# A new order of all pieces of work in a fused attention and MLP kernel

## The chip, the cores and the metric

The kernel runs on one core of a Trainium2 chip. The time is the device time of one execution in microseconds (us); the lowest, the median and the highest of three runs are given. A core has five engines with a queue of instructions each: PE (matrix products; its weight loads are listed as PEld), DVE (vector), ACT (scalar functions), POOL and SP, which here only issues transfers. Each engine works through its queue strictly in order, and an instruction that waits for another engine or for a transfer holds up all that stands behind it on its own queue.

## The reference

One normalised input feeds two branches, and their sum is added to the input. The rest of the function is plain: `x` is 2048 x 512, there are 32 heads of 16, and four segments of 512 rows.

```python
xn = _layernorm(x, axis=-1)
return x + _A_ref(xn, A_wq, A_wk, A_wv, A_wo, A_beta) + _B_ref(xn, B_w1, B_w2)

# _A_ref, for each of 4 segments s
logits = jnp.einsum('bhqd,bhkd->bhqk', qs, ks) * scale + mask
a_dot = jnp.einsum('bhqk,bhkd->bhqd', _softmax(logits, axis=-1), vs)
a_mem = (phi(qs) @ M) / (phi(qs) @ z + 1e-06)
o = g * a_mem + (1.0 - g) * a_dot          # g = sigmoid(beta), one number a head
M, z = M + phi(ks)^T @ vs, z + sum(phi(ks))

# _B_ref
out = silu(x @ w1) @ w2                    # 512 -> 1792 -> 512
```

The block above writes the two einsums of the memory branch as products, to be short; `phi(t)` is `t + 1` for positive `t` and `exp(t)` otherwise.

## The kernel before

The program is written as 1,333 small pieces of work, and the string `ORDER` (lines 16 to 90) names them in the order in which they are recorded. No scheduler moves anything afterwards: a word of the string calls one function (the table `PIECES`, lines 839 to 865), and what this function issues goes to the end of the queue of each engine concerned. The order of the string is thus the order on every one of the five queues. The numbers in a word are the segment, then the tile, then the part of it.

The words that matter here:

- `busy44`, `busy6`: products of a zero tile into a bank that nobody reads (line 836).
- `xc`, `xd`, `xs`: row statistics on DVE (lines 281 and 284). For tiles 0 to 3, `xq` is the square root on ACT (line 298) and `xi` the reciprocal on DVE; for the later tiles `xg` takes four roots at once on POOL (lines 292 and 295). `Nv` normalises a tile (line 310).
- `X` and `Xa`/`Xv` turn a normalised tile by PE and copy it out (lines 817 and 823); `XD` turns it by a transfer from SP (line 829).
- `k`, `q`, `v`, `h`: dense products (lines 331 and 333). Each uses one of four banks (`pp`, line 133), held until a copy takes the result out: `ka`, `qa`, `va` on ACT (lines 373, 384 and 391), `kv`, `qv`, `vv` on DVE. A copy of keys is followed by two masked copies on POOL (line 376).
- `S`: the scores of one batch, on PE (line 701), then their exponential on ACT (line 707), then the causal mask on POOL (line 718). There are 72 such batches, one bank group for all of them, so the scores of a batch cannot be written before the exponential of the one before has read them.
- `E` and `O`: weighted values on PE (line 763). `h`, `ha`, `hv`: the MLP's first product, its tanh (line 477) and its gating (line 482). `o`, `oc`, `od`, `oh`: the output product in whole, half and quarter width; `st` and `sh` add the input and store (lines 606, 611, 653 and 657).
- `tb`: one exponential of a single column (line 304). `tanh`: the tanh of `beta_r`, 128 x 1, on ACT (line 244), which waits for the transfer that loads `beta_r`. `gate`: one small operation on DVE that reads its result (line 247); what comes out is first used by `w` (line 535), far later.
- `lw0`, `lw1`: the loads of `w2` and `wo`, issued by ACT (line 168). `xl`: the reload of an input tile for the final addition, issued by SP (line 599).

The loads of the start are not in the string. They are issued ahead of it, in the order of lines 163 to 180: four tiles of `x` (two by ACT), then by SP `wv` in two halves, `wk`, `wq`, `x` tiles 4 to 7, `w1`, `x` tiles 8 to 11, `x` tiles 12 to 15, and last `beta_r`, 128 elements of 2 bytes.

Of the kernel before, what the change touches and what calls it, by code (L numbers as in the profile page):

```python
# [16 lines left out]
kind odd omask ones0 ones1 zeros xc0 xd0 xc1 xq0 xi0 Nv0 busy44 xd1 xq1 xc2 xi1 X0.1 Nv1 xd2 Xa0.1 busy6 v0.0.0 v0.0.1 xq2 X1.1 Xa1.1 xs3 v0.0.2 v0.0.3 xq3 v0.1.0 xi2 v0.1.1 v0.1.2 v0.1.3 Nv2 xi3 X2.1 va0.0 va0.1 Nv3 Xv2.1 X3.1 Xv3.1 tb k0.1.0 k0.0.0 k0.0.1 k0.0.2 k0.0.3 ka0.0 fp0.0 q0.0.0 q0.0.1 fa0.0 q0.0.2 q0.0.3 k0.1.1 k0.1.2 k0.1.3 qa0.0 k0.3.0 ka0.1 fa0.1 fp0.1 q0.1.0 q0.1.1  # L17
S0 q0.3.0 q0.3.1 k0.3.1 q0.1.2 q0.1.3 q0.3.2 xs6 xs5 k0.3.2 qa0.1 xs7 q0.3.3 xs4 xg4.4 k0.3.3 kv0.3 fv0.1
S2 q0.2.0 q0.2.1 q0.2.2 q0.2.3 qv0.2 h0.5.0 h0.5.1 qv0.3 h0.5.2 h0.5.3 ha0.5 Nv6 h0.11.0 XD6
S1 h0.11.1 hv0.5 v0.3.0 v0.3.1 v0.3.2 Nv5 v0.3.3 vv0.3 h0.11.2 h0.11.3 Nv7 XD5 ha0.11 hv0.11 k0.2.0 h0.10.0 xs9  # L20
S3 XD7 v0.2.0 v0.2.1 Nv4 XD4 h0.10.1 h0.10.2 fp0.3 v0.2.2 h0.10.3 k0.2.1 k0.2.2 ha0.10 bmask v0.2.3 vv0.2
S4 v1.2.0 v1.2.1 fv0.0 k0.2.3 kv0.2 v1.2.2 v1.2.3 hv0.10 v1.1.0 vv1.2 v1.1.1 v1.1.2 v1.1.3 fa0.2
S7 v1.3.0 v1.3.1 xs11 vv1.1 h0.13.0 h0.13.1 h0.13.2 h0.13.3 fp0.2 E0 xs10 Ev0 ha0.13 hv0.13 xs8 xg8.4
# [6 lines left out]
S13 k1.0.0 k1.0.1 k1.0.2 k1.3.2 k1.3.3 kv1.3 q1.3.0 q1.3.1 q1.3.2 Nv8 k1.0.3 tanh ha0.12 t0.1  # L30
S12 gate h0.9.0 h0.9.1 XD10 kv1.0 h0.9.2 h0.9.3 gp1.1 k1.1.0 k1.1.1 ha0.9 Nv11 XD11 hv0.12 k1.1.2 k1.1.3 XD8 q1.3.3
S15 h1.11.0 h1.11.1 h1.11.2 h1.11.3 ha1.11 qv1.3 hv0.9 m0.2 mv0.2 kv1.1 E2 Ev2 h1.9.0
S17 m0.0 mv0.0 h1.9.1 h1.9.2 h1.10.0 h1.10.1 xs15 h1.10.2 h1.10.3 h1.9.3 ha1.9 hv1.11 hv1.9
S21 O2 Ov2 xs14 xg12.4 h0.0.0 h0.0.1 h0.0.2 h0.0.3 ha0.0 k2.2.0
S14 hv0.0 k2.2.1 kv2.2 h0.3.0 h0.3.1 h0.3.2 h0.3.3 ha1.10 o0.2.5 o0.2.11 o0.2.7 Om1
# [879 lines left out]
```

## Time and profile before

| | |
|---|---|
| time, three runs | 222.64, 222.67 (median), 223.12 us |
| span of the profiled execution, first to last instruction | 221.5 us |
| what lies around the span, median less span | 1.2 us |
| instructions | 9,380 |
| DVE busy | 182.4 us (82%) |
| ACT busy | 185.0 us (84%), of it the 72 exponentials of line 707: 135.1 us |
| POOL busy | 134.9 us (61%) |
| transfers | 19.61 MB, mean 89 GB/s |

The profiled execution has no time of its own beside its span; the 1.2 us between the span and the median of the runs are carried along as they are.

A row of the timeline gives the start (us from the span's start), the duration, the engine, the line, the operation, what it writes and reads, and, in brackets, how long the engine had stood idle before it and what ended this. Rows of one kind that follow each other are merged with their count. On SP and on the queues marked q, the duration is that of the issuing, not of the transfer. Ends of matrix products are modelled, so spacings of starts are more to be trusted than durations. In a row of stretches each engine has its busy time and, in brackets, its instructions; behind them stand the granted clock of PE, the busy share of the 16 transfer engines and what they moved.

### The profile page before, as it was taken

The page shows a single profiled execution, that of the slowest core. Times are in us where ns is not written, and L with a number is a line of the kernel's source. Part 1 is how long each engine was busy: PE and PEld are TensorE (multiplying, and loading weights), DVE is VectorE, ACT ScalarE, POOL GpSimd, SP SyncE. Part 2 cuts the span into 40 slices and gives each one's busy share as a digit, 9 for nine tenths or more (in the row PEclk, how much of TensorE's full clock was granted, in tenths as well). Part 3 has the DMA queues.
Part 4 walks back from the last instruction along what each step waited for, and adds up shares of the span by engine and source line. Part 5 has one row for each costly group of instructions (what it writes and reads, how often), then busy time and mean ns, then how long its engine had stood idle before and what let it go on. Part 6 is the DMA issues. An engine that isn't in the chain of part 4 may idle for free.

```text
span 221.5 us, 9380 instructions
## 1 busy us (share of the span) xinstructions
PE 214.9 (97%) x4027; PEld 117.3 (53%) x4027; DVE 182.4 (82%) x367; ACT 185.0 (84%) x174; POOL 134.9 (61%) x253
## 2 busy tenths in 40 slices
PE   8999999999999999999999999999999999999993
PEld 8676555646554444455444444555454554565652
DVE  7678999898869979798887989877898889578833
ACT  3799999899999999999989999999999998952000
POOL 6079779599868695976776786792745472510000
PEclk9999999999999999999999999999999999999999
DMA  6993319922003320621432122220042210303223
GB/s 192 365 385 85 68 34 326 79 55 46 4 13 113 97 50 26 101 51 29 110 92 79 37 66 60 51 73 7 3 128 84 84 51 14 113 28 106 66 74 96
DMA packets 32746, 19.61 MB, mean 89 GB/s; under 512 B 14656, under 2 KB 32192, under 8 KB 32704
## 3 DMA queue, kind: packets, MB, share of 16 engines
q1 hardware_dynamic: 30080, 16.39, 28.8%
q10 hardware_dynamic: 2624, 2.62, 3.6%
q8 instruction: 31, 0.51, 1.0%
q14 instruction: 11, 0.09, 0.2%
HBM read 9.96 MB, written 2.10 MB: 54 GB/s over the span
## 4 chain that ended last, share of the span: by engine, by line
PE 73%; ACT 8%; DVE 7%; POOL 6%; issue 2%; DMA 1%; POOLq 0%; DVEq 0%
PE ps L331 15%; PE psO L333 15%; PE ps L333 11%; PE psO L331 10%; PE psS L701 8%; PE psV L763 7%; ACT Pb L707 5%; PE psS L333 3%; POOL Pb L718 3%; PE psS L836 2%; POOL lows L718 1%; DVE xn_t L310 1%; DVE stats L281 1%; DVE hT L482 1%; DVE Vz L391 1%
## 5 line engine op out<-in xcount | busy, mean ns | idle before, releaser
L707 ACT ACTIVATE Pb<-psS 128x2048 bf16<-128x2048 f32 x72 | 135.1, 1877 | 6.6 <-PE psS L701 4.9
L718 POOL TENSOR_SCALAR_AFFINE_SELECT Pb<-Pb 128x256 bf16<-128x256 bf16 (+2 forms) x120 | 67.9, 587 | 15.6 <-ACT Pb L707 12.6
L482 DVE SCALAR_TENSOR_TENSOR hT<-th,ps 128x512 bf16<-128x512 bf16 x56 | 38.0, 679 | 10.5 <-ACT th L477 9.7
L718 POOL TENSOR_SCALAR_AFFINE_SELECT lows<-Pb 64x256 bf16<-64x256 bf16 (+1 forms) x56 | 25.8, 473 | 33.9 <-ACT Pb L707 29.9
L333 PE MATMUL psO<-w_sb,hT 128*32 128x512 bf16 (+2 forms) x636 | 38.8, 325 | 0.0
L477 ACT ACTIVATE th<-ps 128x512 bf16<-128x512 f32 x56 | 33.2, 594 | 4.3 <-PE ps L333 4.0
L333 PE MATMUL ps<-xnT,w_sb 128*32 128x512 bf16 (+1 forms) x576 | 32.1, 343 | 0.0
L331 PE MATMUL ps<-xnT,w_sb 128*128 128x512 bf16 (+1 forms) x136 | 29.1, 331 | 0.0
L333 PEld LDWEIGHTS <-hT 128*32 128x32 bf16 x804 | 19.6, 97 | 13.4 <-issue 2.6
L331 PE MATMUL psO<-w_sb,hT 128*128 128x512 bf16 (+2 forms) x107 | 26.0, 323 | 0.0
L701 PE MATMUL psS<-qT,k 32*128 32x64 bf16 (+3 forms) x512 | 23.0, 233 | 0.5 <-ACT Pb L707 0.3
L763 PE MATMUL psV<-Pb,Vz 128*32 128x448 bf16 (+7 forms) x512 | 21.8, 287 | 0.8 <-POOL Pb L718 0.8
L763 PEld LDWEIGHTS <-Vz 128*32 128x32 bf16 x768 | 16.3, 97 | 10.1 <-issue 2.1
L701 PEld LDWEIGHTS <-k 32*128 32x128 bf16 x512 | 9.4, 92 | 23.0 <-issue 22.1
L333 PEld LDWEIGHTS <-w_sb 128*32 128x32 bf16 x576 | 14.7, 97 | 8.1 <-issue 1.2
L331 PEld LDWEIGHTS <-w_sb 128*128 128x128 bf16 x136 | 12.8, 98 | 9.7 <-issue 1.1
L376 POOL TENSOR_SCALAR k<-kT,pm_odd 128x512 bf16<-128x512 bf16 x16 | 12.2, 764 | 8.7 <-ACT kT L373 7.6
L331 PE MATMUL ps<-xnT,wq_sb 128*128 128x512 bf16 (+1 forms) x71 | 15.4, 332 | 0.0
L701 PE MATMUL psS<-qT,kT 16*128 16x448 bf16 (+3 forms) x256 | 14.7, 269 | 0.0
L331 PEld LDWEIGHTS <-hT 128*128 128x128 bf16 x107 | 9.4, 98 | 10.0 <-issue 2.2
L333 PE MATMUL psO<-wo_sb,oT 128*32 128x512 bf16 x160 | 14.6, 381 | 0.0
L331 PE MATMUL ps<-wv_sb,xnT 128*128 128x512 bf16 x53 | 14.4, 380 | 0.0
(111 smaller groups left out, 325.9 us busy)
## 6 DMA issues: line engine op xcount, KB each, us to landing
spr<-rz SPq DMA_DIRECT2D x56, 64.0 KB
x_res<-in_A_x_dram SPq DMA_DIRECT2D x16, 128.0 KB
out_dram<-o_out SPq DMA_DIRECT2D x15, 128.0 KB
w_sb<-in_B_w_dram SPq DMA_DIRECT2D x1, 1792.0 KB
w_sb<-in_B_w_dram ACTq DMA_DIRECT2D x1, 1792.0 KB
x_hi<-in_A_x_dram SPq DMA_DIRECT2D x2, 512.0 KB
wv_sb<-in_A_wv_dram SPq DMA_DIRECT2D x2, 256.0 KB
wk_sb<-in_A_wk_dram SPq DMA_DIRECT2D x1, 512.0 KB
```

The source lines that it names most:

```text
L281: nc.vector.bn_stats(out=stats[t][:], in_=xs(t, t + 1)[:, 0, :])
L310: eng.tensor_scalar(out=xn[t][:], in0=xs(t, t + 1)[:, 0, :], scalar1=mv_all[:, t, 0:1], scalar2=rstd_all[:, t, 0:1], op0=ALU.subtract, op1 ...
L331: return [nc.tensor.matmul(out, lhsT=lhsT, rhs=rhs, start=start, stop=stop, skip_group_check=True)]
L333: nc.tensor.matmul(out[c : c + 32], lhsT=lhsT[:, c : c + 32], rhs=rhs, start=start, stop=stop, tile_position=(0, c), skip_group_check=True,)
L376: nc.gpsimd.tensor_scalar(out=to, in0=frm, scalar1=keep[:, 0:1], scalar2=1.0, op0=ALU.mult, op1=ALU.mult)
L477: nc.scalar.activation(out=th[:], in_=sts[s]["h", ft][:, :], func=AF.Tanh, scale=0.5)
L482: nc.vector.scalar_tensor_tensor(out=st["hT"][:, ft, :], in0=st.pop(("th", ft))[:], scalar=1.0, in1=st.pop(("h", ft))[:, :], op0=ALU.add, ...
L701: nc.tensor.matmul(psS[:, g, c : c + q2 - q1], lhsT=keys[rows], rhs=st["qT"][rows, dt, q1:q2], start=True, stop=True, tile_position=(32 * ...
L707: exp = nc.scalar.activation(out=Pb[:, :, :], in_=psS[:, :, :], func=AF.Exp, scale=SCALE)
L718: over[id(Pb)].append(nc.gpsimd.affine_select(out=out, in_=in_, compare_op=ALU.is_ge, fill=0.0, base=base, pattern=[[0, out.shape[1]], [1, ...
L763: nc.tensor.matmul(psV[32 * g : 32 * g + 32, q0 : q0 + nq], lhsT=Vzs[s % 2][:, kt, 4 * dt + g, par : par + 2, :].rearrange("p a d -> p (a ...
L836: nc.tensor.matmul(idle[:, 0:P], lhsT=zraw[:, 0:P], rhs=zraw[:, 0:P], start=True, stop=True)
```

## The change

Only the string `ORDER` changes. It holds the same words, with no new piece and none left out; nearly every line has them in another order, and the batches `S` run in another sequence too. Its first line, which holds everything ahead of the first scores, shows the kind:

```diff
-kind odd omask ones0 ones1 zeros xc0 xd0 xc1 xq0 xi0 Nv0 busy44 xd1 xq1 xc2 xi1 X0.1 Nv1 xd2 Xa0.1 busy6 v0.0.0 v0.0.1 xq2 X1.1 Xa1.1 xs3 v0.0.2 v0.0.3 xq3 v0.1.0 xi2 v0.1.1 v0.1.2 v0.1.3 Nv2 xi3 X2.1 va0.0 va0.1 Nv3 Xv2.1 X3.1 Xv3.1 tb k0.1.0 k0.0.0 k0.0.1 k0.0.2 k0.0.3 ka0.0 fp0.0 q0.0.0 q0.0.1 fa0.0 q0.0.2 q0.0.3 k0.1.1 k0.1.2 k0.1.3 qa0.0 k0.3.0 ka0.1 fa0.1 fp0.1 q0.1.0 q0.1.1
+xc0 xd0 ones1 xc1 busy44 tb xq0 xi0 Nv0 X0.1 xd1 xq1 xc2 xi1 xd2 xq2 odd busy6 Nv1 X1.1 Xa0.1 v0.0.0 v0.0.1 v0.0.2 Xa1.1 v0.1.0 v0.1.1 ones0 xs3 xq3 xi2 Nv2 xi3 v0.0.3 va0.0 tanh Nv3 X2.1 Xv2.1 v0.1.2 v0.1.3 va0.1 X3.1 Xv3.1 k0.1.0 k0.0.0 k0.0.1 k0.0.2 k0.0.3 q0.0.0 k0.1.1 q0.0.1 q0.0.2 lw1 q0.0.3 kind gate xs6 ka0.0 fp0.0 xs7 k0.1.2 k0.1.3 xs5 fa0.0 fv0.0 k0.3.0 qa0.0 ka0.1
```

The table below it is replaced in the same way to its end. Three places in the queues are shown.

On ACT, the start of the program, before. `x_lo` are the first input tiles, `spare` and `rstd_all` the one-column square roots, `xnT` the turned input:

```order
L158 DMA x_lo<-in_A_x_dram 128x512 x2
L185 ACT_TABLE_LOAD
L185 ACTIVATE spare<-zraw 128x1
L298 ACTIVATE rstd_all<-mv_all,eps 128x1 x2
L823 COPY xnT<-ptr 128x2x128 x2
L298 ACTIVATE rstd_all<-mv_all,eps 128x1
```

The same place now:

```order
L185 ACT_TABLE_LOAD
L185 ACTIVATE spare<-zraw 128x1
L304 ACT_TABLE_LOAD
L304 ACTIVATE spare<-eps 128x1
L298 ACT_TABLE_LOAD
L298 ACTIVATE rstd_all<-mv_all,eps 128x1 x3
L823 COPY xnT<-ptr 128x2x128 x4
```

The exponential of one column (`tb`) has moved ahead of the square roots, so that a table for it and a second one for the roots are loaded in between.

On ACT, from the value copies (`Vz`) to the first exponential of a batch (`Pb`), before:

```order
L391 CAST Vz_110<-ps 128x16x2x16 x2
L304 ACT_TABLE_LOAD
L304 ACTIVATE spare<-eps 128x1
L373 CAST kT<-ps 128x512
L408 ACTIVATE ex<-kT 128x512
L384 CAST qT<-ps 128x512
L373 CAST kT<-ps 128x512
L408 ACTIVATE ex<-kT 128x512
L707 ACTIVATE Pb_141<-psS 128x2048
```

The same place now:

```order
L391 CAST Vz_110<-ps 128x16x2x16
L244 ACT_TABLE_LOAD
L244 ACTIVATE gate<-beta_r 128x1
L391 CAST Vz_110<-ps 128x16x2x16
L168 DMA wo_sb<-in_A_wo_dram 128x4x512
L373 CAST kT<-ps 128x512
L408 ACTIVATE ex<-kT 128x512
L384 CAST qT<-ps 128x512
L373 CAST kT<-ps 128x512
L707 ACTIVATE Pb_141<-psS 128x2048
```

The tanh of `beta_r` has come from far behind into the gap between the two value copies, and the load of `wo` stands right behind the second of them. All key and query copies and all exponentials are queued behind both.

On DVE, from the copies of the turned input (`xnT`) to the statistics of tiles 4 to 7 (`x_hi`), before:

```order
L823 COPY xnT<-ptr 128x4x128 x2
L281 BN_STATS stats<-x_hi 128x6
L284 BN_AGGR mv_all<-stats 128x2
L281 BN_STATS stats<-x_hi 128x6
L284 BN_AGGR mv_all<-stats 128x2
```

The same place now:

```order
L823 COPY xnT<-ptr 128x4x128 x2
L234 TENSOR_REDUCE kind<-ident 128x1
L238 TENSOR_SCALAR evec<-kind 128x1
L239 TENSOR_SCALAR evec_125<-kind 128x1
L240 TENSOR_TENSOR evec_125<-evec_125,evec 128x1
L241 TENSOR_SCALAR sign<-kind 128x1
L247 TENSOR_SCALAR gate<-gate,sign 128x1
L281 BN_STATS stats<-x_hi 128x6
L284 BN_AGGR mv_all<-stats 128x2
```

The operation on `gate`, which reads what the tanh on ACT writes, now stands ahead of the statistics of the later tiles; before, it stood behind more than 80 rows of DVE.

More of the change, by code (lines that the diff above doesn't have):

```diff
@@ L19 @@
[L19 to L23, printed above, removed]
@@ L30 @@
[L30 to L35, printed above, removed]
@@ new lines @@
+S1 qv0.2 hv0.5 h0.11.0 h0.11.1 v0.3.0 v0.3.1 v0.3.2 v0.3.3 Nv4 h0.11.2 h0.11.3 ha0.11 xs9 fp0.1 k0.2.0 Nv7
+S3 h0.10.0 hv0.11 h0.10.1 k0.2.1 h0.10.2 h0.10.3 ha0.10 vv0.3 XD4 v0.2.0 v0.2.1 xs8 k0.2.2 k0.2.3
+S4 v1.2.0 v1.2.1 v1.2.2 v1.2.3 kv0.2 fp0.2 XD7 hv0.10 v0.2.2 fv0.1 v1.1.0 v1.1.1 v1.1.2 h0.13.0 fa0.2
+S5 v0.2.3 vv1.2 xs10 h0.13.1 h0.13.2 h0.13.3 ha0.13 vv0.2 v1.1.3 vv1.1 E0 k1.2.0
+S8 k1.2.1 Ev0 hv0.13 k1.2.2 v1.3.0 k1.2.3 v1.0.0 h0.1.0 xs11 xg8.4 kv1.2 v1.0.1 v1.0.2 fa0.3 v1.0.3
+S11 fv0.2 t0.2 h0.1.1 h0.1.2 v1.3.1 v1.3.2 v1.3.3 h0.1.3 ha0.1 lw0 xs14 vv1.0 O0
@@ new lines @@
+S12 omask h0.9.1 h0.9.2 h1.11.0 h1.11.1 Nv9 hv0.12 h0.9.3 Nv8 XD8 ha0.9 k1.1.0 k1.1.1 k1.1.2 XD9 k1.1.3 kv1.1
+S17 h1.11.2 hv0.9 Om0 q1.3.0 q1.3.1 q1.3.2 q1.3.3 qv1.3 h1.11.3 ha1.11 E2 Ev2 m0.2
+S15 mv0.2 h1.9.0 h1.9.1 h1.9.2 h1.9.3 hv1.11 h0.0.0 ha1.9 O2 Ov2 h1.10.0 hv1.9 Om2
+S16 h0.0.1 h1.10.1 h1.10.2 h1.10.3 h0.0.2 m0.0 Nv13 mv0.0 h0.0.3 k2.2.0 ha0.0 hv0.0
+S14 h0.3.0 h0.3.1 h0.3.2 h0.3.3 Om1 bmask k2.2.1 kv2.2 gp1.1 h0.6.0 ha1.10 h0.6.1 h0.6.2 h0.6.3 hv1.10 ha0.3
+S21 q2.1.0 q2.1.1 hv0.3 qv2.1 ha0.6 O3 Ov3 E3
@@ new lines @@
+S22 o0.2.4 h1.8.0 od0.2.0.1 Nv12 o0.2.1 h1.8.1 h1.8.2 h1.8.3 hv0.6 od0.2.0.2 Ev3 oc0.2.9.1 ha1.8 gv1.1 hv1.8 k2.1.0
+S18 xl0.0 k2.1.1 v2.1.0 v2.1.1 kv2.1 gp1.2 gp1.0 ga1.2 sv0 r0.3 h1.0.0 h1.0.1 o0.2.6 XD13 r0.0
+S19 r0.1 r0.2 w0 z0.3 v2.2.0 o0.2.11 h1.0.2 h1.0.3 ha1.0 v2.2.1 vv2.2 o0.2.3 o0.2.8 hv1.0
+S20 Om3 oc0.2.9.0 h1.5.0 z0.2 h1.5.1 h1.5.2 h1.5.3 ha1.5 vv2.1 q2.3.0 oc0.2.2.0 q2.3.1 qv2.3
+S24 fa1.3 z0.0 k2.0.0 k2.0.1 hv1.5 E4 Ev4 kv2.0 zv0.2 h1.4.0 h1.4.1 gv1.2 od0.2.0.0
+S25 zv0.3 h1.4.2 h1.4.3 ha1.4 o0.2.10 hv1.4 o0.2.12 q2.0.0 q2.0.1 qv2.0 o0.0.6 XD12
@@ new lines @@
+S23 od0.0.11.0 o0.2.16 z0.1 o0.0.1 zv0.1 ga1.0 gv1.0 o0.0.3 o0.0.9 o0.2.7 O4 o0.2.17
+S26 o0.0.16 fp1.0 h1.1.0 xl0.2 o0.2.13 h1.1.1 h1.1.2 h1.1.3 od0.0.11.3 fp1.3 oc0.0.13.1 od0.0.11.2 o0.0.5 oc0.2.2.1 ha1.1 od0.2.0.3
+S27 Ov4 oc0.0.4.0 h1.12.0 h1.12.1 o0.2.5 h1.12.2 hv1.1 zv0.0 h1.12.3 ha1.12 E5 Ev5 o0.0.15
+S28 oc0.0.13.0 o0.0.7 o0.2.15 o0.0.8 hv1.12 o0.2.14 mw0.2 h1.13.0 h1.13.1 O5 fa1.0 Nv14
+S31 o0.0.0 st0.2 h1.13.2 Ov5 k2.3.0 k2.3.1 kv2.3 o0.0.10 fv1.3 h1.13.3 ha1.13 h1.6.0
+S29 o0.3.4 hv1.13 od0.3.10.1 o0.0.2 h1.6.1 oc0.0.4.1 o0.0.14 fp1.2 Om5 o0.0.12 h1.6.2 h1.6.3 XD14 od0.0.11.1 ha1.6 h1.3.0 xl0.1
@@ new lines @@
+S40 o0.1.7 o0.1.0 o0.3.12 o0.1.1 O7 ga2.2 oc0.3.13.1 Ov7 o0.3.8 m1.2 mv1.2
+S36 o0.3.9 Om7 o1.2.3 o1.2.1 xl1.2 s1 oc0.3.11.1 o0.3.15 o0.3.16 o0.3.5 od0.3.10.3 fp2.1 gv2.2 o0.3.2 st0.3 od1.2.5.1
+S37 sv1 r1.1 o1.2.8 oc0.1.12.0 o1.2.2 r1.0 o0.1.11 o1.2.6 q3.1.0 q3.1.1 qv3.1 gp2.1 fa2.1 xl1.0 oc0.1.12.1 st0.1
+S41 k3.1.0 q3.3.0 q3.3.1 r1.2 r1.3 w1 z1.3 o1.2.4 d1.2 ga2.1 qv3.3 v2.3.0
+S47 k3.1.1 z1.0 kv3.1 d1.3 v2.3.1 vv2.3 h2.8.0 h2.8.1 ha2.8 fv2.1 t2.1 oc1.2.0.0 q3.2.0 hv2.8 gv2.1
+S38 oc1.2.10.1 ga2.3 E8 Ev8 k3.0.0 k3.0.1 q3.2.1
@@ new lines @@
+S42 kv3.0 m1.0 mv1.0 dv1.2 v3.3.0 fp2.2 v3.3.1 qv3.2 h2.0.0 z1.2 Om6 vv3.3 h2.0.1 ha2.0 h1.7.0
+S39 dv1.3 h1.7.1 hv2.0 v3.0.0 v3.0.1 vv3.0 h1.7.2 h1.7.3 zv1.3 gp2.3 E9 ha1.7 hv1.7
+S48 fa2.2 q3.0.0 q3.0.1 qv3.0 o1.2.11 Ev9 v3.2.0 v3.2.1 d1.1 vv3.2
+S43 n1.3 nv1.3 h2.4.0 h2.4.1 k3.2.0 k3.2.1 fv2.2 kv3.2 ha2.4
+S45 fp2.3 h2.7.0 gv2.3 z1.1 hv2.4 h2.7.1 O8 fp2.0 Ov8 ha2.7 hv2.7 oc1.2.0.1 o1.2.7 dv1.1 d1.0 o1.0.3 od1.2.5.2
+S44 o1.0.10 oc1.2.10.0 o1.0.1 h2.11.0 h2.11.1 fa2.0 zv1.2 od1.0.5.3 n1.2 nv1.2 ha2.11 o1.0.12 o1.0.13 od1.2.5.0 zv1.0
@@ new lines @@
+S49 o1.0.6 hv2.11 h2.3.0 h2.3.1 o1.0.8 O9 fv2.0 o1.0.11 Om8 Ov9 od1.0.5.2 ha2.3 dv1.0 t2.0
+S46 oc1.0.4.1 o1.0.7 oc1.0.9.0 h2.2.0 h2.2.1 ha2.2 t2.2 od1.0.5.0 fa2.3 hv2.3 mw1.2 v3.1.0 zv1.1 o1.0.2
+S51 v3.1.1 od1.2.5.3 o1.0.16 hv2.2 o1.2.13 vv3.1 n1.0 nv1.0 od1.0.5.1 o1.0.17 oc1.0.9.1 gp2.0 o1.2.17 E10 Ea10
+S50 o1.2.16 mw1.0 n1.1 ga2.0 k3.3.0 k3.3.1 o1.2.14 nv1.1 xl1.3 fv2.3 o1.2.9 kv3.3 o1.2.15 t2.3 o1.2.12
+S53 O10 Ov10 o1.0.0 h2.1.0 h2.1.1 o1.0.14 oc1.0.4.0 st1.2 gv2.0 ha2.1 o1.3.6
+S52 o1.0.15 E11 hv2.1 ga3.0 oc1.3.10.1 o1.3.5 st1.0 h2.13.0 h2.13.1 ha2.13 o1.3.14 Om9 Ev11 m2.2 mv2.2 gp3.0
@@ new lines @@
+S64 oc2.0.6.0 hv3.1 gv3.3 d2.1 o2.0.14 O13 Ov13 h3.8.0 h3.8.1 ha3.8 hv3.8 o2.2.8
+S67 o2.2.11 o2.0.10 oc2.0.2.1 n2.3 o2.2.9 h3.12.0 h3.12.1 ha3.12 od2.0.7.2 nv2.3 s3 dv2.1 od2.0.7.0 od2.0.7.1 sv3
+S68 o2.2.17 hv3.12 od2.2.6.2 n2.1 nv2.1 o2.2.14 o2.2.12 h3.2.0 h3.2.1 ha3.2 E14 hv3.2 Ea14
+S66 o2.0.9 o2.0.17 o2.2.2 od2.2.6.0 n2.2 nv2.2 h3.11.0 h3.11.1 o2.0.4 Om13 ha3.11 xl2.0 r3.2 o2.2.15
+S65 hv3.11 o2.3.10 o2.2.4 o2.2.16 st2.2 o2.3.5 h3.6.0 h3.6.1 r3.3 o2.1.15 ha3.6 hv3.6
+S69 o2.0.1 o2.0.15 o2.1.4 o2.0.16 st2.0 o2.3.6 oc2.3.13.1 o2.1.14 O14 r3.0
```

85 lines of the change are left out of this document (24 added, 61 removed).

## The prediction

> **What bounds the kernel now.** First the page's head and the chain of waits, then stretches of the span.
>
> ```profile
> span 221.5 us, 9380 instructions
> PE 214.9 (97%) x4027; PEld 117.3 (53%) x4027; DVE 182.4 (82%) x367; ACT 185.0 (84%) x174; POOL 134.9 (61%) x253
> PE 73%; ACT 8%; DVE 7%; POOL 6%; issue 2%; DMA 1%; POOLq 0%; DVEq 0%
> ```
>
> ```profile
> 10.00:60.00 50.00, 48.24 (x867) 29.69 (x869) 44.69 (x90) 47.87 (x46) 40.02 (x72) 1.00 0.54 128
> 60.00:210.00 150.00, 149.84 (x2896) 75.38 (x2888) 125.37 (x243) 132.20 (x117) 91.42 (x167) 1.00 0.24 64
> ```
>
> PE (first figure of a stretch) works 149.84 of 150 us from 60 on, and 48.24 of 50 before. The number of products is that of the words, which stay the same, so PE's work cannot shrink: a time lost on PE early is lost for good, and what an order can win is the idle time alone. The waits of PE list it:
>
> ```profile
> PE psS L836 <- DVE zraw L183: 1.1, 1, 1.1
> PE psV L763 <- POOL Pb L718: 0.8, 2, 0.6
> PE ps L333 <- DMA xnT<-xn_t: 0.4, 1, 0.4
> PE psS L701 <- ACT Pb L707: 0.3, 1, 0.3
> PE ps L331 <- DVE kT L373: 0.3, 1, 0.3
> ```
>
> The first row is the very start. The other four make **1.8 us**: all that a perfect order could take out between the start and the end. So the start and the end decide, and there the change does something large.
>
> **The change at the start: a wait for beta_r.** The tanh of `beta_r` now stands on ACT between the two value copies. Where was it, and when does what it reads land?
>
> ```profile
> L244 ACT ACTIVATE gate<-beta_r x1: 195/195/195, 46.2 to 46.2; 128x1 f32<-128x1 bf16 x1
> 6.47 2.08 SPq L158 DMA_DIRECT2D x_end<-in_A_x_dram  x1
> 8.59 3.93 SPq L178 DMA_DIRECT2D beta_r<-in_A_beta_dram  x1
> 0.00:18.00 18.00, 16.51 (x154) 13.43 (x155) 13.05 (x41) 12.88 (x22) 8.78 (x25) 1.00 0.89 306
> 18.00:19.00 1.00, 1.00 (x23) 0.59 (x21) 0.74 (x3) 1.00 (x3) 0.90 (x2) 1.00 0.08 23
> 19.00:20.00 1.00, 1.00 (x8) 0.51 (x6) 1.00 (x3) 1.00 (x1) 1.00 (x2) 1.00 0.00 0
> ```
>
> Before, the tanh ran at 46.2 and took 0.195 us; nothing was late. `beta_r` is the last load that SP issues, at 8.59. The issuing took 3.93 us, so it cannot have landed before 12.5. The stretches say when the loads were through: 306 GB/s over 18 us are 5.51 MB, and the issued inputs add up to 5,376 KB = 5.51 MB; between 18 and 19 the rate is 23 GB/s, then zero until the first turning transfer. A second row shows the lag of that queue:
>
> ```profile
> 3.76 0.51 SPq L158 DMA_DIRECT2D x_hi<-in_A_x_dram  x1
> 11.28 0.69 DVE L281 BATCH_NORM_STATS2 stats<-x_hi 128x6 f32<-128x512 bf16 x1 [1.06 <-DMA x_hi<-in_A_x_dram]
> ```
>
> DVE had to wait until 11.28 for a load issued at 3.76, 7.5 us later. For `beta_r` I take the end of the traffic, **18.9 us**; bounds 12.5 and 19.2. The loads and their order on SP are the same in the changed kernel, and ACT has no load ahead of the tanh.
>
> [...] The early landing is a rival below.
>
> **What stands behind the tanh.** On ACT: the second value copy, the `wo` load, then all key and query copies and exponentials. Their durations and starts before:
>
> ```profile
> 9.24 0.59 ACT L391 CAST Vz<-ps 128x512 bf16<-128x512 f32 x1 [0.19 <-PE ps L331]
> 9.84 1.28 ACT L304 ACT_TABLE_LOAD   x1
> 11.25 0.57 ACT L373 CAST kT<-ps 128x512 bf16<-128x512 f32 x1
> 11.85 0.63 ACT L408 ACTIVATE ex<-kT 128x512 bf16<-128x512 bf16 x1
> 12.38 0.57 ACT L384 CAST qT<-ps 128x512 bf16<-128x512 f32 x1
> 12.85 0.59 ACT L373 CAST kT<-ps 128x512 bf16<-128x512 f32 x1
> 14.01 1.86 ACT L707 ACTIVATE Pb<-psS 128x2048 bf16<-128x2048 f32 x1
> 13.14 0.21 PE L701 MATMUL psS<-qT,k 32*128 32x64 bf16 x4
> ```
>
> Now: landing 18.9, tanh to 19.15, value copy 0.6 to 19.75, key copy from 19.75 (11.25 before), exponential 20.35, query copy 20.9 to 21.45. The scores need that query copy and the masked keys of POOL. Before, the query copy ended at 12.95 and the scores started at 13.14 behind POOL's second masked copy; the batch that is now first reads POOL's first one alone, so I set the scores at query copy plus 0.05: **21.5 instead of 13.14, +8.4 us**. PE has dense products ahead of these scores, but they are soon done: 26 of 256 columns, against 30 before. It owes 4 of them, at 0.11 us (below), **+0.4 us**. PE cannot run ahead further: its third key tile needs the bank of the second value copy, and the scores stand in its queue.
>
> **The extra table loads** (1.28 us each, row above) do not add to this. Two more stand ahead of the first root; before, ACT had an idle gap there:
>
> ```profile
> 4.55 0.29 ACT L298 ACTIVATE rstd_all<-mv_all,eps 128x1 f32<-128x1 f32 x1 [1.33 <-DVE mv_all L284]
> ```
>
> 2 x 1.28 and the 0.2 us exponential less 1.33 make the first root some 1.4 us later, and the first products about 2 us. Then the first value copy ends near 11 and the tanh is reached near 12.3. All of it lies under the wait to 18.9. Without that cover it would cost about 1.6 us on PE.
>
> **DVE** stands at `gate` until about 19.2, with the statistics of tiles 4 to 7 behind it. Four of them at 0.69 plus 0.18 and the roots of POOL put the first turning transfer about 6.5 us after 19.2; before, it was issued at 19.32, 6.2 us after the first scores. The values that need it come behind the fifth batch, some 9.6 us after the first scores (batches 2.4 us apart: 14.01, then 16.36). I cost it at nothing; its cover is those 3 us. **The `wo` load**, formerly at 67, meets empty queues at 20 (row 19:20 above): nothing.
>
> **PE's clock.** From about 14.5 to 21.5 PE has nothing but two products. What an idle spell does, this trace shows only at the start:
>
> ```profile
> 1.10 4.88 PE L836 MATMUL psS<-zraw 128*128 128x128 bf16 x44 [1.10 <-DVE zraw L183]
> 6.20 0.70 PE L836 MATMUL psS<-zraw 128*128 128x128 bf16 x6
> 17.13 1.04 PE L331 MATMUL ps<-xnT,w_sb 128*128 128x256 bf16 x8
> ```
>
> 44 products of 128 columns took 4.88 us, 0.11 us each; later 256 columns take the same 0.11 (1.04 us, less 0.27 for the last one's depth, over 7). So PE ran at half its rate until about 6.2, though the clock column says 1.00. If it falls back in a pause of 5 to 7 us, it loses half of up to 5.1 us: **bounds 0 and 2.6**. I take **+2.0**, near the only row there is, as part of the slow stretch may lie under waits.
>
> [...]
>
> **What the order may win.** Of the 1.8 us of PE's waits I take half, **-0.9** (bounds -1.8 and, if new waits come, +1.5). At the end:
>
> ```profile
> 216.70 0.69 DVE L606 SCALAR_TENSOR_TENSOR o_out<-psO,x_res 128x512 bf16<-128x512 f32 x1 [0.28 <-PE psO L333]
> 217.45 0.50 PE L333 MATMUL psS<-wo_sb,oT 128*32 128x256 bf16 x12
> 218.64 0.42 DVE L653 SCALAR_TENSOR_TENSOR o_half<-psS,x_res 128x256 bf16<-128x256 f32 x1 [0.86 <-DMA out_dram<-o_out]
> ```
>
> PE ends at 217.95, the last half addition waits until 218.64 for an output buffer that a store still reads, and 3.5 us after PE all is over. Now a whole tile comes last, 3 us of products behind the store that frees its buffer, so that wait goes: 0.69 for the addition and the 2.4 us from 219.06 to the end make 3.1, **-0.4**.
>
> **Sum:** 221.5 + 8.4 + 0.4 + 2.0 - 0.9 - 0.4 = 231.0 us of span. Plus the 1.2 us between this span and the median of the runs: **232.2 us**, +4.3%.
>
> **Rivals.**
> - *The pause, but no slow restart.* For it: no row shows PE falling back within the program. Against: the start. 232.2 - 2.0 = 230.2. Chance 0.2.
> - *The pause, and what follows it stands worse.* DVE and POOL start with a backlog, the turning transfers come after the values want them, and the order, laid out without the pause, meets new waits: +1.5 in place of -0.9, so 234.6. For it: DVE is 89% busy in 10 to 60 (44.69 of 50). Chance 0.14.
> - *beta_r lands early* (the other side). If it is there when ACT comes to the tanh, about 12.3, the first exponential slips from 14.01 only to 15.1. This +1.1, less 1.8 and 0.4, gives 221.6, faster. It decides at the landing: up to some 13.4 the gains cover the delay. For it: SP is done with the issuing at 12.5. Against: the traffic goes on to 18, and 7.5 us of lag on the same queue. Chance 0.04, of it half within the bound.
> - *My forecast,* 231 to 233.5: chance 0.62.
>
> Range: the forecast and its two slower-or-equal neighbours, 229.4 to 234.6. Faster by over 0.2% (about what a measurement of this kernel can tell from no change): 0.02; within: 0.02; slower: 0.96.
>
> **What would show it.** Right: on ACT a wait of some 6 us for the transfer of `beta_r`, tanh at 19; DVE's `gate` behind it; the first scores at 21.5; products after that spaced 0.2 us for 256 columns for some microseconds, then 0.11; behind 60 the same full PE. Each step fails by its own row: a tanh at 13 kills the pause, a spacing of 0.11 right after it the restart, new waits of PE behind 60 the -0.9, and an end more than 3.3 us behind PE's last product the -0.4. The prediction is wrong altogether if the first scores start before 17.

## The result and the profile after

| | before | after |
|---|---|---|
| median | 222.82 us (222.64 to 223.12, 4 runs) | 236.7 us (235.3 to 237.84, 4 runs) |
| profiled execution: own time, span | span 221.5 us | 237.63 us, span 235.9 us |
| start of the first scores | 13.14 us | 21.99 us |
| from there to the end of PE's last product | 204.8 us | 210.2 us |
| from there to the end of the span | 3.5 us | 3.7 us |

The changed kernel takes 1.0614 times as long (95% interval 1.0565 to 1.0664), 13.9 us more. Single executions of e1 (356.23 us), e3 (239.55 us), e10 (767.89 us, its profiled one) and the kernel before (353.83 us) fell into a slower state of the chip and count in no time or ratio below. The page's head of the changed kernel, with busy times, PE's busy tenths and granted clock over 40 slices, and the chain of waits:

```profile
PE 216.4 (92%) x4010; PEld 119.1 (50%) x4033; DVE 179.4 (76%) x367; ACT 188.0 (80%) x176; POOL 136.2 (58%) x253
PE   6753999999989999999989999999997999999993
PEclk9795699999999999999999999999999999999999
PE 66%; SPq 10%; DMA 10%; DVE 7%; issue 3%; ACT 3%; DVEq 0%; ACTq 0%
```

PE is busy as long as before (216.4 against 214.9 us) but 92% of the span instead of 97%: the new time is waiting. The gap is in the first four slices (PE), and the clock was down in slice 2 and again in slices 4 and 5 (PEclk). The dip of slice 2 lies ahead of the pause: from 7.5 to 10.5 the mean clock is 0.50, while e3, with the same words there, has 1.00. In the chain, SP's queue and the transfers have 10% each. The start, row by row in the timeline:

```profile
9.40 3.86 SPq L178 DMA_DIRECT2D beta_r<-in_A_beta_dram  x1
11.88 1.28 ACT L244 ACT_TABLE_LOAD   x1
14.15 0.60 PE L331 MATMUL ps<-xnT,wk_sb 128*128 128x256 bf16 x4
19.64 0.20 ACT L244 ACTIVATE gate<-beta_r 128x1 f32<-128x1 bf16 x1 [6.48 <-DMA beta_r<-in_A_beta_dram]
19.75 0.57 ACT L391 CAST Vz<-ps 128x512 bf16<-128x512 f32 x1
19.87 0.21 DVE L247 TENSOR_SCALAR gate<-gate,sign 128x1 f32<-128x1 f32 x1 [6.66 <-ACT gate L244]
20.36 0.58 PE L331 MATMUL ps<-xnT,wk_sb 128*128 128x256 bf16 x2 [5.61 <-ACT Vz L391]
21.99 0.62 PE L701 MATMUL psS<-qT,k 32*128 32x64 bf16 x8 [1.04 <-ACT qT L384]
24.21 1.92 PE L331 MATMUL ps<-xnT,wq_sb 128*128 128x256 bf16 x8
27.84 1.04 PE L331 MATMUL ps<-xnT,wq_sb 128*128 128x256 bf16 x8
29.32 1.34 SPq L829 DMA_TRANSPOSE xnT<-xn_t  x1
```

ACT reaches the tanh at 13.2, waits 6.48 us for `beta_r`, and the value copy behind it frees PE's bank only at 20.3. DVE's `gate` waits as long. The two rows of eight equal products show the clock: 1.92 us at 24.21, 1.04 us at 27.84. PE's longest waits, but for the 1.1 us of the very start, are of another kind than before:

```profile
PE ps L331 <- ACT Vz L391: 5.6, 1, 5.6
PE ptr L817 <- DVE xn_t L310: 2.3, 2, 2.0
PE psS L701 <- ACT qT L384: 1.0, 1, 1.0
PE ps L331 <- DVE o_out L606: 0.9, 1, 0.9
PE ps L333 <- DVE o_out L606: 0.9, 1, 0.9
```

The first three rows are the start. The two rows for `o_out` lie far behind it, where PE formerly did not stop. (Gaps of 0.2 us that the list puts down to "issue", 1.3 us in all, are read as missing records: the page has 4,010 products for 4,033 weight loads, and e1's trace has 4,033 products.) One stretch of windows for the same piece of the span as in the prediction:

```profile
60.00:210.00 150.00, 145.51 (x2810) 74.23 (x2818) 121.23 (x237) 140.82 (x123) 101.97 (x185) 1.00 0.23 53
```

PE had 149.84 of these 150 us before and has 145.51 now. Even without the gaps of missing records, the new order is less dense on PE long after the start, and this the forecast did not have.

### The profile page after: what moved, and what is told of

Same layout as the page of the kernel before. It is cut to its first block, busy times and chain, and to the rows that moved or that the text cites. A ratio compares the mean times of both kernels' runs of the same rounds, so it can differ in the third digit from the quotient of the medians.

```text
span 235.9 us, 9379 instructions
## 1 busy us (share of the span) xinstructions
PE 216.4 (92%) x4010; PEld 119.1 (50%) x4033; DVE 179.4 (76%) x367; ACT 188.0 (80%) x176; POOL 136.2 (58%) x253
## 3 DMA queue, kind: packets, MB, share of 16 engines
q1 hardware_dynamic: 30080, 16.39, 27.8%
## 4 chain that ended last, share of the span: by engine, by line
PE 66%; SPq 10%; DMA 10%; DVE 7%; issue 3%; ACT 3%; DVEq 0%; ACTq 0%
PE ps L331 22%; PE ps L333 12%; PE psS L701 9%; PE psO L333 9%; PE psV L763 6%; PE psO L331 6%; SPq L562 4%; DMA beta_r<-in_A_beta_dram 4%; DMA spr<-rz 3%; SPq L158 2%; ACT Pb L707 2%; DMA x_res<-in_A_x_dram 1%; SPq L168 1%; SPq L785 1%; DVE ri L530 1%
## 5 line engine op out<-in xcount | busy, mean ns | idle before, releaser
L333 PE MATMUL psO<-w_sb,hT 128*32 128x512 bf16 (+2 forms) x656 | 41.8, 324 | 0.0
L331 PE MATMUL ps<-xnT,w_sb 128*128 128x256 bf16 (+1 forms) x149 | 31.7, 326 | 0.9 <-issue 0.5
L333 PE MATMUL ps<-xnT,w_sb 128*32 128x512 bf16 (+1 forms) x512 | 30.0, 348 | 1.0 <-DVE o_out L606 0.9
L331 PE MATMUL psO<-w_sb,hT 128*128 128x512 bf16 (+2 forms) x94 | 24.2, 319 | 0.5 <-issue 0.3
L331 PE MATMUL ps<-xnT,wk_sb 128*128 128x512 bf16 (+1 forms) x66 | 15.6, 344 | 5.9 <-ACT Vz L391 5.6
L331 PEld LDWEIGHTS <-w_sb 128*128 128x128 bf16 x152 | 14.2, 98 | 9.8 <-issue 1.5
L333 PEld LDWEIGHTS <-w_sb 128*32 128x32 bf16 x512 | 13.5, 96 | 10.5 <-issue 3.0
L333 PE MATMUL psO<-wo_sb,oT 128*32 128x512 bf16 x172 | 15.9, 380 | 0.5 <-DVE oT L593 0.5
L701 PE MATMUL psS<-qT,kT 16*128 16x64 bf16 (+3 forms) x256 | 14.9, 272 | 0.0
L331 PE MATMUL ps<-xnT,wq_sb 128*128 128x256 bf16 (+1 forms) x58 | 13.8, 360 | 1.1 <-DVE o_out L606 0.9
```

The lines of the kernel that those rows point to most:

```text
L331: return [nc.tensor.matmul(out, lhsT=lhsT, rhs=rhs, start=start, stop=stop, skip_group_check=True)]
L333: nc.tensor.matmul(out[c : c + 32], lhsT=lhsT[:, c : c + 32], rhs=rhs, start=start, stop=stop, tile_position=(0, c), skip_group_check=True,)
L701: nc.tensor.matmul(psS[:, g, c : c + q2 - q1], lhsT=keys[rows], rhs=st["qT"][rows, dt, q1:q2], start=True, stop=True, tile_position=(32 * ...
```

## The experiments

All edits are of the string `ORDER` unless said otherwise; a diff shows the words next to the moved one. Ratios are to the kernel before, measured beside each.

**e1: the tanh and the gate late again**

```diff
-va0.0 tanh Nv3
+va0.0 Nv3
-q0.0.3 kind gate xs6
+q0.0.3 kind xs6
-S9 ha0.12
+S9 tanh ha0.12
-S12 omask
+S12 gate omask
```

> The changed order, with the tanh of beta_r and its operation on DVE alone put back to where they stood before, behind the fourteenth batch. Theory 1, the wait for beta_r and the slow restart of PE make most of the loss: the first scores start near 14.8 us instead of 21.99 (the table loads still cost about 1.6), no half rate of PE after the start, so 236.7 - 7.2 - 2.3 = about 227.2 us. Theory 2, the rest of the order (table loads, later waits) makes most of the loss: 232 us or more.

227.81 us, ratio 1.0231 (1.0198 to 1.0265). By the ratios 8.5 of 13.7 us go with two words. The first scores start at 15.18, still 2 us late, and PE's two waits for `o_out` stay. The timeline of e1 shows what lies behind one of them:

```profile
157.80 6.64 SPq L562 DMA_DIRECT2D spr<-rz  x10
164.48 0.46 SPq L599 DMA_DIRECT2D x_res<-in_A_x_dram  x1
167.78 0.69 DVE L606 SCALAR_TENSOR_TENSOR o_out<-psO,x_res 128x512 bf16<-128x512 f32 x1 [1.48 <-DMA x_res<-in_A_x_dram]
```

SP issues ten spreads in a row, 6.64 us, and the reload that DVE will want stands behind them.

**e2: beta_r loaded early, the order as changed.** The load moves from the end of SP's start loads (line 178) to just behind the first input tiles.

```diff
+    nc.sync.dma_start(
+        out=beta_r[:], in_=bass.AP(tensor=A_beta.tensor, offset=A_beta.offset, ap=[[1, H], [0, 4], [1, 1]])
+    )
     load_w(nc.sync, wv_sb, A_wv, 0, 2)
```

> The changed order as it is, but the load of beta_r is issued by SP right behind the first input tiles instead of last. Theory 1: the tanh finds its data, ACT does not wait near 12, the first scores start near 15 us, about 227 us. If the tanh or its table load is what costs and not the late landing: 236 to 237 us as in the changed kernel.

227.77 us, ratio 1.0204 (1.0174 to 1.0234), with the tanh at its early place:

```profile
12.22 1.28 ACT L244 ACT_TABLE_LOAD   x1
13.52 0.20 ACT L244 ACTIVATE gate<-beta_r 128x1 f32<-128x1 bf16 x1
```

No wait is left at the tanh. So it is the late landing of `beta_r`, and not the tanh's place in itself, that costs.

**e3: PE kept busy in the pause.** A hundred products of zeros into the bank that nobody reads, ahead of the product that waits.

```diff
-fv0.0 k0.3.0
+fv0.0 busy100 k0.3.0
```

> The changed order with 100 more products of a zero tile (128 columns) ahead of PE's third key tile, where PE stands still for 5.8 us. Nothing else moves. If the half rate of PE after 22 us comes from the pause: the products there are spaced 0.11 us per 256 columns instead of 0.21, and the time falls by 2.3 us to about 234.4. If the half rate has another cause: 236.7 us as before, or a little more for the added products.

234.84 us, ratio 1.0531 (1.0492 to 1.0569). One stretch of windows, of the changed kernel and of e3 (behind the five busy times stand PE's clock, the transfers' share and GB/s):

```profile
22.00:28.00 6.00, 6.00 (x40) 3.53 (x40) 2.27 (x7) 3.73 (x4) 4.33 (x8) 0.52 0.15 53
```

```profile
22.00:28.00 6.00, 6.00 (x76) 4.46 (x69) 4.57 (x12) 5.99 (x7) 5.37 (x9) 1.00 0.14 45
```

The first scores start at the same time (21.88), but PE now gets 76 products through in these 6 us instead of 40. From the first scores to PE's last product e3 takes 207.4 us instead of 210.2, so the half clock is worth 2.8 us in the traces (2.7 by the first three exponentials, below); the ratios differ by 0.0083, about 1.9 us, with an uncertainty of some 1.4. Part of the gain is lost at e3's end, where a reload comes 2.69 us late.

**e4: the kernel before, with only the tanh and the gate early**

```diff
-va0.0 va0.1
+va0.0 tanh va0.1
-q0.3.2 xs6
+q0.3.2 gate xs6
-k1.0.3 tanh ha0.12
+k1.0.3 ha0.12
-S12 gate h0.9.0
+S12 h0.9.0
```

> The kernel before with one part of the change alone: the tanh of beta_r between the two value copies and its operation on DVE ahead of the statistics of tiles 4 to 7; all else as before. Theory 1: ACT waits near 11 to 19.5 us, the first scores start near 21.5 instead of 13.14 (+8.4), PE restarts at half rate (+2.3): 222.8 + 10.7 = about 233.5 us. Theory 2: 223 to 226 us.

232.52 us, ratio 1.0437 (1.0414 to 1.0459). Timeline of e4:

```profile
20.04 0.20 ACT L244 ACTIVATE gate<-beta_r 128x1 f32<-128x1 bf16 x1 [10.10 <-DMA beta_r<-in_A_beta_dram]
20.77 0.58 PE L331 MATMUL ps<-xnT,wk_sb 128*128 128x256 bf16 x2 [8.46 <-ACT Vz L391]
```

Two words moved in a steady order cost 9.7 us. First scores at 22.6 instead of 13.1, +9.5; PE's last product 9.3 later. The half clock that follows here too (mean of the run 0.976) leaves no trace in the sum.

**e5: the kernel before, with only `tb` early**

```diff
-xc1 xq0 xi0
+xc1 tb xq0 xi0
-Xv3.1 tb k0.1.0
+Xv3.1 k0.1.0
```

> The kernel before with the first exponential of one column alone moved ahead of the square roots, so that ACT loads two more tables at the start. If the start of the changed order is late because of the table loads: the first root 1.4 us later, the first scores near 14.7 us instead of 13.14, 222.8 + 1.6 = 224.4 us. If ACT's idle time at the start hides them: within 0.4 us of 222.8.

225.43 us, ratio 1.0161 (1.0129 to 1.0192), 3.6 us. The timeline of e5:

```profile
4.80 1.28 ACT L298 ACT_TABLE_LOAD   x1
6.10 0.30 ACT L298 ACTIVATE rstd_all<-mv_all,eps 128x1 f32<-128x1 f32 x1
```

The root comes at 6.10 instead of 4.55, and the first scores 1.95 us later (15.08). Two loads of 1.28 us now stand ahead of it, the second as shown. They are a real cost, covered in the changed kernel by the longer wait. The times show more than the 1.95 us; of the rest no row is known.

**e6: the changed kernel, with tanh, gate and `tb` at their old places.** As e1, and:

```diff
-busy44 tb xq0
+busy44 xq0
-xs6 ka0.0
+xs6 tb ka0.0
```

> The changed order with the tanh and its operation on DVE put back as in e1, and the first exponential put back ahead of the key copies as well. By the table loads: 1.6 us below e1 (228.4), so 226.8; if another part of the new start makes the first scores of e1 late (15.18 against 13.14), the time stays at 228.

224.49 us, ratio 1.0117 (1.0089 to 1.0146). First scores at 12.97, earlier than in the kernel before. All that is left of the loss is behind them: 206.6 us to PE's last product instead of 204.8. In this execution 1.2 us of that is a wait for the landing of `w1`, at 18.4. The timeline of e6 shows another place (the last bracket is PE's wait):

```profile
98.66 6.10 SPq L426 DMA_TRANSPOSE phiK<-pk  x4
104.86 1.08 SPq L785 DMA_DIRECT2D zraw<-oraw  x2
107.10 0.48 DVE L807 COPY_PREDICATED oraw<-omask,odd 128x256 int32<-128x256 int32 x1 [1.98 <-DMA zraw<-oraw]
109.24 1.02 PE L331 MATMUL ps<-xnT,wq_sb 128*128 128x512 bf16 x4 [0.94 <-DVE o_out L606]
```

Four turning transfers of `phiK` take SP 6.10 us to issue. The small transfer of `oraw` goes out only behind them, DVE waits 1.98 us for it, and PE 0.94 for what DVE has behind it. In the kernel before, these transfers were issued one at a time, 1.2 to 2.0 us each, with others in between; two rows of its SP queue:

```profile
99.94 1.21 SPq L426 DMA_TRANSPOSE phiK<-pk  x1
103.31 1.09 SPq L785 DMA_DIRECT2D zraw<-oraw  x2
```

**e7: e6 with the late wait moved on DVE and one reload ahead of the spreads**

```diff
-o0.3.9 Om7 o1.2.3
+o0.3.9 o1.2.3
-st0.3 od1.2.5.1
+st0.3 Om7 od1.2.5.1
-o1.3.16 s2 sv2
+o1.3.16 xl1.1 s2 sv2
-od1.3.12.0 xl1.1 dv2.3
+od1.3.12.0 dv2.3
```

> e6 with two pieces moved that wait for SP's queue: the reload of an input tile ahead of the ten spreading transfers that it stood behind, and one merge on DVE behind the store that it held up. If the two waits of 0.94 and 0.85 us on PE (110.8 and 168.5 in e1) come from SP's queue as the trace has it: both gone, e6 less 1.8 us, about 225. If only passed on: as e6.

223.68 us, ratio 1.0068 (1.0042 to 1.0093). The reload's wait near 168 is gone. The other one was only passed on, as the timeline of e7 shows:

```profile
108.09 0.48 DVE L516 SCALAR_TENSOR_TENSOR zsum<-ps,evec,zraw 128x256 f32<-128x256 f32 x1 [0.86 <-DMA zraw<-odd]
110.17 1.02 PE L331 MATMUL ps<-xnT,wq_sb 128*128 128x512 bf16 x4 [0.95 <-DVE qT L384]
```

With the waiting instruction moved, the next one in line waits for the next transfer of the same late queue; the four turning transfers still stand ahead, in 6.29 us. That points at SP's queue; e9 tests it.

**e8: the kernel before, the half additions in buffers that nobody reads any more** (the wait at the end that the forecast spoke of; line 652).

```diff
-        o_half = work.tile([P, D], BF16, name="o_half", tag="o_out", bufs=3)[:, 0 : D // 2]
+        o_half = work.tile([P, D], BF16, name="o_half", tag="odd", bufs=2)[:, 0 : D // 2]
```

> The kernel before with one edit of its own: the two last half tiles are added up in buffers that are free by then, instead of those that a store still reads. If the 0.86 us wait of DVE at the end is on the path: 222.8 - 0.6 = 222.2 us, faster than both kernels. If the transfers of the stores end last anyway: 222.8.

222.06 us, ratio 0.999 (0.9972 to 1.0008): no change that can be told. In its trace the end behind PE's last product shrinks from 3.5 to 2.9 us, as expected, but the times do not confirm a gain of that size.

**e9: e6 with the cause on SP taken away.** The reload as in e7, and two of the four turning transfers behind the transfers of `oraw` and `odd`.

```diff
-S35 t1.0 o0.3.3
+S35 o0.3.3
-fv1.1 t1.1 h1.2.2
+fv1.1 h1.2.2
-Ov7 o0.3.8
+Ov7 t1.0 t1.1 o0.3.8
-o1.3.16 s2 sv2
+o1.3.16 xl1.1 s2 sv2
-od1.3.12.0 xl1.1 dv2.3
+od1.3.12.0 dv2.3
```

> The changed kernel with tanh, gate and tb back at their old places (as in e6_tanh_tb_back, 224.5 us), and three words moved in the later order: xl1.1 (the reload of x) ahead of the spreads s2, and two of the four block transposes of phiK (t1.0, t1.1) from ahead of the odd rows' products to behind Ov7. In e6 the four transposes held SyncE's queue 6.1 us (98.66 to 104.76), the load of oraw was issued only behind them, and VectorE waited 1.9 us for it, and TensorE 0.94 us for VectorE. Theory (the new order's later waits are the backlog of SyncE's queue): the load goes out about 3 us sooner, both waits of TensorE on o_out (0.9 and, in e1, the one near 168) go, 222.7 us (222.2 to 223.3), as before within 0.3%. Rival (the waits are passed on to the next consumer, as in e7, because VectorE itself is late): 223.7, with a wait of TensorE of 0.9 or more between 105 and 115.

223.06 us, ratio 1.003 (1.0006 to 1.0054). Timeline of e9 at the same place:

```profile
97.36 2.50 SPq L426 DMA_TRANSPOSE phiK<-pk  x2
101.31 1.08 SPq L785 DMA_DIRECT2D zraw<-oraw  x2
103.75 0.44 DVE L807 COPY_PREDICATED oraw<-omask,odd 128x256 int32<-128x256 int32 x1
```

`oraw` goes out at 101.31, DVE's merge has no wait any more, and PE's list has neither of the two waits for `o_out` that e1 and the changed kernel have. From the first scores to PE's last product it is 204.4 us, against 204.8 in the kernel before. The step from e6 to e9 holds a caveat: e9's profiled execution has no wait for `w1`, which lies far ahead of the moved words, so not all of the difference between these two need be SP's. The comparison of e1 and e9 below is free of it.

**e10 and e11: the kernel of e4, with PE kept busy in the wait**

```diff
-qa0.0 k0.3.0
+qa0.0 busy150 k0.3.0
```

> The kernel before with tanh and gate alone at the early place (as in e4_before_tanh_early, 232.5 us), and 150 products of zeros put into TensorE's queue ahead of k0.3.0, where it waits 8.46 us for Vz; they take some 8 us at full clock. Theory (the idle wait is what brings the half clock, and the half clock costs what the products take longer): the granted clock stays full, the first scores stay at 22.6, and the stretch from the first scores to TensorE's last product falls below e4's 204.65 by 2.0 to 2.6: 230.2 us. Rival (on this order the half clock lies beside slack of the early stages and costs nothing): clock full and 232.5 again. Rival two (the half clock comes from something else than the idle TensorE): the half clock stays and the time with it.

232.55 us, ratio 1.0456 (1.0429 to 1.0483), with a mean clock of 1.0 in four of the five runs behind these figures and 0.993 in the fifth, against 0.976 to 0.978 in e4. The clock stayed up and the time did not fall. To see it in a trace, e11 has `busy135`:

> As e10_before_wait_filled (the kernel before with tanh and gate alone early, and products of zeros in TensorE's wait), with 135 of them instead of 150: by the 5.75 us that 100 took in e3_busy_in_pause they last 7.8 us and end inside e4's wait of 8.46 us. e10 ran as long as e4 with the granted clock full. Theory (on the order of before the half clock lies beside slack of the first stages, which are not held by TensorE there): clock full, first scores at 22.6, and from there to TensorE's last product 204.6 as in e4 (204.65) and before (204.82): 232.5 us. Rival (e10's 150 products ran 0.2 us into the work behind them, and their own cost hid the gain): the stretch falls to 202.5 and the time to 230.3.

232.41 us, ratio 1.0476 (1.0427 to 1.0525). In the timeline of e11 the wait of 8.46 us is filled but for small rests:

```profile
12.04 7.70 PE L836 MATMUL psS<-zraw 128*128 128x128 bf16 x135
20.46 0.38 PE L331 MATMUL ps<-xnT,wk_sb 128*128 128x256 bf16 x2 [0.72 <-ACT Vz L391]
21.04 0.60 PE L331 MATMUL ps<-xnT,wq_sb 128*128 128x256 bf16 x4 [0.20 <-ACT kT L373]
22.30 0.21 PE L701 MATMUL psS<-qT,k 32*128 32x64 bf16 x4 [0.67 <-POOL k L376]
```

Its profiled execution still had a short time at half clock behind these rests, but two of its four runs had a mean clock of 0.999 and 1.0 and took 232.84 and 231.72 us, where a gain of 2 us on e4's 232.52 would have shown. On the order of before, half clock behind the pause costs nothing that these runs can tell; on the changed order it costs 2 to 3 us (e3). One profiled execution of each shows how: from the first exponential of a batch to the second, e4 needs 0.83 us more than the kernel before, but to the eleventh 0.37 us less, so what the half clock took is won back within ten batches. In the changed kernel nothing is won back (next table). Why the one order has this slack and the other not was not settled.

**The parts side by side**, as ratios to the kernel before, with 222.8 us:

| kernel | ratio | left of the loss | what the step took away |
|---|---|---|---|
| after | 1.0614 | 13.7 us | |
| e1: tanh and gate back | 1.0231 | 5.1 us | 8.5 us |
| e6: `tb` back too | 1.0117 | 2.6 us | 2.5 us |
| e9: and three words for SP's queue | 1.0030 | 0.7 us | 1.9 us |

The intervals are 1.1 us to each side in the first row and 0.5 to 0.8 in the others; the 0.7 us left at the end are 0.1 to 1.2. No version here beats the kernel before.

The traces give the same parts in another way. The changed kernel, e1 and e9 run the 72 exponentials of line 707 in the same sequence. This is how long after the first of them a later one starts, in us, in one profiled execution of each:

| exponential | after | e1 | e9 | after less e1 | after less e9 |
|---|---|---|---|---|---|
| 3rd | 7.64 | 5.18 | 5.18 | 2.46 | 2.46 |
| 16th | 39.23 | 36.75 | 36.78 | 2.48 | 2.45 |
| 17th | 42.66 | 40.22 | 39.46 | 2.44 | 3.20 |
| 39th | 95.61 | 93.18 | 92.42 | 2.43 | 3.19 |
| 41st | 101.57 | 99.14 | 97.18 | 2.43 | 4.39 |
| 61st | 154.19 | 151.78 | 149.80 | 2.41 | 4.39 |
| 63rd | 160.35 | 157.89 | 154.68 | 2.46 | 5.67 |
| 72nd | 183.51 | 181.03 | 177.83 | 2.48 | 5.68 |

Against e1, which has no pause, the changed kernel loses 2.5 us ahead of the third exponential and nothing more up to the last. e3, which has the pause but not the half clock, is level with e1 up to the twelfth. So behind the first scores the pause costs what the half clock costs: these 2.5 us, and 0.2 more between the first scores and the first exponential. Against e9 the changed kernel and e1 both lose 1.2 us between the 39th and the 41st, where the four turning transfers stand ahead of `oraw`, and 1.3 between the 61st and the 63rd, where the reload stands behind the ten spreads. The 0.75 us at the 17th are in these two and not in e6, which has the same words there as e1; their cause was not looked for.

## Why the prediction was right in its direction and too small

The median of 236.7 us lies 4.5 us above the 232.2 of the forecast and above its range.

**The wait for `beta_r`: right, and a little short.** The forecast put the landing at 18.9 and the first scores at 21.5, +8.4. The tanh started at 19.64, the scores at 21.99: +8.85. The traffic itself ended as forecast: 25 GB/s between 18.5 and 19 us, then none. The tanh started 0.6 us behind that end, a lag that the forecast put at nothing. When the load was issued did not decide: 9.40 here and 8.42 in e3, where the tanh still started at 19.53. e2 settles the rival that the load lands early: it did not, and where it does, the wait is gone. e4 shows the wait alone, without the rest of the new order.

**The four products owed: as forecast.** 26 products of 256 columns were done ahead of the first scores. The premise that the number of products stays the same is off by a trifle: 4,033 in e1's trace for 4,027 before, since a dense product goes as one instruction or as four narrow ones by its neighbours in the order (lines 330 and 882), and two more now go as four.

**The table loads: hidden in the changed kernel, as forecast, but under-priced without the cover.** The forecast had 1.6 us; the traces have 1.95 (e5) and 2.2 (15.18 in e1 against 12.97 in e6), the ratios 2.5 (e1 to e6) and 3.6 (e5). It matters as soon as somebody mends the tanh alone.

**DVE's backlog: right that it costs PE nothing at the turning transfers.** The first is issued at 29.32, 7.3 us behind the first scores, and PE's list has no wait for one; by the forecast it would have come at about 25.7. Nor did the backlog cost anything indirectly up to the last exponential: behind the third, the changed kernel keeps pace with e1, which has no such backlog.

**The half clock: right that it comes, and near in size.** Forecast +2.0; 2.7 to 2.8 by the traces and about 1.9 by the times of e3. The rival without a slow restart falls. But the price is not general, as e4, e10 and e11 show.

**What the order may win, -0.9: the step that failed.** The forecast took half of PE's 1.8 us of waits as gained and allowed new waits up to +1.5. The waits of before largely went, and others took their place. Span against span, the stretch from the first scores to PE's last product grew by 5.4 us; less 0.4 for the products owed and 2.8 for the half clock, **+2.2** is left instead of -0.9. This 3.1 us is most of the miss. The failed step is that the sum counted the idle time that the new order drops and put nothing against it for the waits that the order itself makes. In e9, where two of these are gone, the stretch is 204.4 us with the four products still owed, so the order does gain some 0.8 us there, close to the 0.9. The rival with +1.5 had the sign, but named the backlog of DVE and POOL and the turning transfers of tiles as its cause, which the pace of e1 rules out. The runs show another: SP's queue, in whose order the prediction looked at the start alone. The same two places as in e1 and e6 stand in the timeline of the changed kernel, with the late waits of DVE and PE:

```profile
109.66 5.99 SPq L426 DMA_TRANSPOSE phiK<-pk  x4
115.74 1.08 SPq L785 DMA_DIRECT2D zraw<-oraw  x2
118.03 0.54 DVE L807 COPY_PREDICATED oraw<-omask,odd 128x256 int32<-128x256 int32 x1 [1.91 <-DMA zraw<-oraw]
120.24 1.02 PE L331 MATMUL ps<-xnT,wq_sb 128*128 128x512 bf16 x4 [0.95 <-DVE o_out L606]
...
167.23 6.64 SPq L562 DMA_DIRECT2D spr<-rz  x10
173.91 0.46 SPq L599 DMA_DIRECT2D x_res<-in_A_x_dram  x1
177.28 0.69 DVE L606 SCALAR_TENSOR_TENSOR o_out<-psO,x_res 128x512 bf16<-128x512 f32 x1 [1.53 <-DMA x_res<-in_A_x_dram]
178.02 1.05 PE L333 MATMUL ps<-xnT,w_sb 128*32 128x512 bf16 x16 [0.91 <-DVE o_out L606]
```

They are 0.95 and 0.91 us of PE's idle time, 1.2 and 1.3 us by the exponentials, and e9 removed both by three words. They do not come from the pause: e1 has no pause and has both. Of the other waits of the list, 0.9 us in two rows not shown here lie with DVE and 0.5 us in one with ACT; they were not tried.

**The end, -0.4: wrong in sign.** The end grew from 3.5 to 3.7 us. The wait for an output buffer is gone, as forecast, and a later reload took its place, which the forecast did not look for:

```profile
231.80 0.82 DVE L653 SCALAR_TENSOR_TENSOR o_half<-psS,x_res 128x256 bf16<-128x256 f32 x2 [1.81 <-DMA x_res<-in_A_x_dram]
```

In spans: 0.5 for the scores, 0.8 for the clock, 3.1 for the new waits and 0.6 for the end make, but for rounding, the 4.9 from 231.0 to 235.9. The 1.2 us around the span were also not what they seemed: executions with both figures have 1.7 (237.63 less 235.9), so the profiled execution of before was one of about 223.2; and that of the changed kernel took 0.9 us more than its median.

## What to carry to other kernels

A word moved in a hand-made order is to be priced at what it waits for and not at what it takes: a tanh of 0.2 us cost 9.7 us because the 128 numbers that it reads were the last of 5.5 MB of loads to be issued. Check a new order on the transfer queue as on the engines, from start to end: here bursts of issuing (6.0 us for four turning transfers, 6.6 for ten spreads) made the small transfers behind them late; moving the instruction that waited passed the wait on (e7), and dividing the burst, or putting the small transfer ahead of it, ended it (e9). And an idle gain is only half a forecast: count what the new order makes late, not only the waits it drops.

## What was not expected of the hardware

- The granted clock stayed at half well after PE had work again. Two stretches of the changed kernel's windows:

```profile
13.00:17.50 4.50, 1.75 (x17) 1.43 (x15) 0.21 (x2) 0.16 (x1) 0.00 (x0) 1.00 1.04 366
17.50:21.50 4.00, 0.58 (x2) 0.11 (x1) 1.57 (x4) 1.83 (x5) 0.60 (x1) 0.51 0.33 62
```

  With the row 22:28 above (0.52), the clock is full through the first 2.7 us of the pause, from 14.75 to 17.5, and half up to about 27.8 (eight products from 27.84 take 1.04 us again, against 1.92 from 24.21), 5.8 us after the first scores. What sets the moments of the fall and of the return, these runs do not show. The length of the longest rest alone does not: in e11 rests of 0.72, 0.20 and 0.67 us stood ahead of the stretch below at 0.77, while e3's single wait of 1.24 us ahead of its first scores was followed by 1.00 (row 22:28 above):

```profile
22.50:30.00 7.50, 7.45 (x72) 4.96 (x67) 4.36 (x11) 6.18 (x7) 6.40 (x12) 0.77 0.00 0
```

- A load of 128 numbers of 2 bytes, issued last behind the big ones of the same queue, let the tanh start 10.2 us after its issue in the changed kernel (9.40 to 19.64) and 11.1 us in e3 (8.42 to 19.53); issued right behind the first input tiles (e2), it was there before 13.5.
